# First loads of an attention and soft-MoE kernel: two q transfers from ScalarE's DMA queue, and GpSimd's first transfer ahead of the identity and the masks

## The chip, the cores and the metric

The kernel runs on one NeuronCore of a Trainium2 chip. The metric is the device time of one execution in microseconds, as the median of several runs. The engines go by the names of the profile: PE is the matrix engine (TensorE), DVE is VectorE, ACT is ScalarE, POOL is GpSimd and SP is SyncE. SP, ACT and POOL can each issue DMA transfers; a transfer that converts fp32 into fp16 on its way is issued by POOL here.

## The reference

The inputs q, k and v have the shape [8, 8, 576, 64] (batch, heads, tokens, head dimension) in fp32. First comes causal attention in a window of 64 tokens, then a soft mixture of 8 experts with 4 slots each over the 4608 tokens of width 512.

```python
# attention
scores = scale * np.matmul(q, k.transpose(0, 1, 3, 2))
mask = (rel >= 0) & (rel < window)
scores = np.where(mask, scores, -1000000000.0)
scores = scores - np.max(scores, axis=-1, keepdims=True)
attn = np.exp(scores)
attn = attn / (np.sum(attn, axis=-1, keepdims=True) + 1e-09)
x = np.matmul(attn, v)                      # then laid out as [4608, 512]
# soft MoE
logits = x @ phi                            # phi [512, 32]
d = softmax of logits over the tokens       # dispatch
slot_input = d.T @ x                        # [32, 512], 4 slots for each of 8 experts
h = np.maximum(slot_input[e] @ w1[e], 0.0)  # w1 [8, 512, 1024]
slot_out[e] = h @ w2[e]                     # w2 [8, 1024, 512]
c = softmax of logits over the slots        # combine
out = c @ slot_out                          # [4608, 512] fp32
```

## The kernel before

The whole program is written out by hand in the order in which each engine is to run it (a manual schedule); the framework adds the semaphores. Each engine works through its own queue strictly in order.

The attention goes over 32 pairs of heads (8 batches of 4 pairs). A pair p passes through a pipeline of stages in the loop `for n in range(-1, NP - 1)` at line 553:

- q and k of the pair are transposed by PE (`st_transpose`, line 316) and copied out of PSUM, k by ACT (line 327) or DVE (line 324), q by ACT (line 336), and in the very first pair half of q by DVE (line 333).
- `st_max` (lines 346 and 349) makes masked scores from which DVE takes the row maxima (line 353); `st_shift` (lines 366 and 367) turns the maxima around; `st_score` (lines 372 and 375) makes the scores with the maxima taken off, and ACT takes the exponential (line 381).
- `st_av` (line 405) multiplies by v, DVE normalises (line 415), and the result is transposed again (lines 429 and 433) for the logits, the softmax over tokens that runs along from batch to batch, and the slot inputs.

After the last pair come the two layers of the experts (`first`, line 816, and `second` and `second_last`, lines 837 and 846), in two halves of 256 output columns. The second half of line 846 needs `w2h`, the last weights to be loaded. Then the output is put together from the combine weights, scaled by ACT and DVE (lines 899 and 897), and written by SP in 14 transfers (line 901).

**The loads.** POOL issues nearly all of them, each one converting fp32 into fp16: k and q in groups of four heads (`load_k`, `load_q`, line 79, group g), v (line 173), and the weights of the experts one by one in between (lines 133, 135, 142, 150 and 155). Their order is written out: `load_k(1)` at line 121, then `load_q(1)`, `load_v(0)`, `load_k(2)` and so on from line 194, and one or more in each step n of the loop. POOL also shifts v for the odd blocks (lines 180 and 182) and writes the 0/1 identity `ident_h` (by `make_identity`) and the two selections that make the mask block `wb` (lines 117 and 119).

The first four heads of q and k (group 0) go another way. They are loaded as fp32 by SP, in four transfers of two heads each (line 103), into memory that will hold weights only later, and are rounded to fp16 by ACT and DVE (`round_rows`, line 110). Each of the four has 96 partitions of two rows of 1536 bytes. The order of issue is k pair 0, q pair 0, k pair 1, q pair 1, and behind them SP issues phi (line 254). The rounding is spread over two engines: ACT rounds k of pair 0 and q of pair 1, DVE rounds q of pair 0 and k of pair 1. On DVE the order is: q of pair 0, the two copies that make `wm` from the mask block (line 233), k of pair 1 and then its half of q (line 333).

ACT's own work begins with the load of its function table, put ahead of its first copy, which writes `lh` (line 211). That copy reads `db`, which DVE makes from the identity (lines 205 to 209).

Of the kernel before, what the change touches and what calls it, by code (L numbers as in the profile page):

```python
# [18 lines left out]
def kernel(  # L19
# [10 lines left out]
    nc = tc.nc  # L30
# [37 lines left out]
    RP = S // RQ  # L68
# [6 lines left out]
    def load_rows(src, g, tag, pairs=(0, 1)):  # L75
        t = pin.tile([128, 4, RQ * Dh], FP16, name=tag, tag=tag)
        b, gq = divmod(g, 2)
        h0, nh = 4 * gq + 2 * pairs[0], 2 * len(pairs)
        nc.gpsimd.dma_start(out=t[0:RP, 0:nh, :],  # L79
                            in_=src[b].rearrange("h (p r) d -> p h (r d)", p=RP)[:, h0:h0 + nh, :])  # L80
        for i, pr in enumerate(pairs):
            staged[tag, 2 * g + pr] = t, 2 * i

    def load_k(g):
        load_rows(k, g, "ks")
# [14 lines left out]
    for i, (src, tag, pr) in enumerate(((k, "ks", 0), (q, "qs", 0), (k, "ks", 1), (q, "qs", 1))):  # L100
        f = w1_t[5 - i // 2, 0][:, :, :].rearrange("p c f -> p (c f)").bitcast(FP32)
        f = f[0:RP, 768 * (i % 2):768 * (i % 2) + 768].rearrange("p (h x) -> p h x", h=2)
        nc.sync.dma_start(out=f, in_=src[0].rearrange("h (p r) d -> p h (r d)", p=RP)[:, 2 * pr:2 * pr + 2, :])
        if pr == 0:
            staged[tag] = pin.tile([128, 4, RQ * Dh], FP16, name=tag, tag=tag)
        first_rows[tag, pr] = f
        staged[tag, pr] = staged[tag], 2 * pr

    def round_rows(tag, pr, copy):
        copy(out=staged[tag][0:RP, 2 * pr:2 * pr + 2, :], in_=first_rows[tag, pr])  # L110

    ident_h = const.tile([128, 128], FP16, name="ident_h")
    nc.vector.memset(ident_h, 0.0)
    wb = const.tile([64, 128], FP16, name="wb")
# [3 lines left out]
                            base=0, pattern=[[1, 128]], channel_multiplier=-1)  # L118
    nc.gpsimd.affine_select(out=wb, in_=wb, compare_op=ALU.is_ge, fill=NEG,
                            base=64, pattern=[[-1, 128]], channel_multiplier=1)  # L120
    load_k(1)


    def w1_dram(e):
# [552 lines left out]
    b, p = B - 1, NP - 1  # L677
# [273 lines left out]
```

## Time and profile before

| | us |
|---|---|
| median of 3 runs | 191.47 |
| lowest and highest run | 191.35, 192.05 |
| profiled execution, whole time | 191.22 |
| profiled execution, span from first to last instruction | 189.4 |
| busy in the span: PE | 160.4 |
| busy in the span: ACT | 144.9 |
| busy in the span: DVE | 142.9 |
| busy in the span: POOL | 98.5 |

The span is what the profile's views count in; the rest of an execution's time lies around it. The mean TensorE clock that was granted is 0.974 of full speed. In the timeline, each line has the start in us, the duration in us, the engine, the line of the kernel, the operation with what it writes and reads, how often it was merged, and in brackets how long the engine had been idle before it and what ended that wait. In the view of busy time by stage a line has the stretch, its length, the busy time of PE, PE's weight loads, DVE, ACT and POOL with the number of instructions, and then the clock, the mean share of the 16 DMA engines' time that packets took (above 1 where packets overlap on an engine) and the rate in GB/s. In the view of DMA queues, a line has the number of packets that started in the stretch, their megabytes, and the time they took as a share of 16 engines' time; `hardware_dynamic` is the queue that SP issues to, `software_dynamic` POOL's.

### The profile page before, as it was taken

What the parts mean: (1) busy time and instruction counts of PE and PEld (TensorE: products, weight loads), DVE (VectorE), ACT (ScalarE), POOL (GpSimd) and SP (SyncE); (2) the same over time, 40 slices, a digit from 0 to 9 for tenths busy, and PEclk for the clock granted to TensorE, in tenths of its full rate; (3) what the DMA queues carried; (4) which work ended last, traced back from release to release, by engine and by line L of the source; (5) the groups of instructions that cost most, each with busy time, mean ns of one, the idle gap of its engine ahead of it and who ended that gap; (6) DMA issues with size and microseconds to landing.
All of it is one profiled execution on the core that took longest, in us unless ns stands there. A gap on an engine that the chain in (4) does not pass through costs nothing. (4 is left out here: it accounts for less than half of the span.)

```text
span 189.4 us, 7060 instructions
## 1 busy us (share of the span) xinstructions
PE 160.4 (85%) x3036; PEld 120.5 (64%) x3036; DVE 142.9 (75%) x352; ACT 144.9 (76%) x266; POOL 98.5 (52%) x123
## 2 busy tenths in 40 slices
PE   5787999999999999999999899999989897769500
PEld 1466878877777777777777787776774365633100
DVE  6798796897888889788878988888886555289800
ACT  6487879989889898988999898988588256379600
POOL 7857927273695554983984828727854160000000
PEclk9999999999999999999999999999999999999955
DMA  6999999999999999999999999999999999979996
GB/s 153 222 184 185 226 175 223 179 223 179 185 226 180 210 192 184 207 196 185 210 195 192 211 182 198 199 204 195 213 214 212 204 196 179 277 258 422 415 415 252
DMA packets 61630, 41.47 MB, mean 219 GB/s; under 512 B 38816, under 2 KB 57504, under 8 KB 60704
## 3 DMA queue, kind: packets, MB, share of 16 engines
q0 software_dynamic: 56560, 30.35, 116.1%
q1 hardware_dynamic: 5040, 10.68, 15.9%
q8 instruction: 23, 0.38, 0.7%
q14 instruction: 7, 0.06, 0.1%
HBM read 61.93 MB, written 9.44 MB: 377 GB/s over the span
## 5 line engine op out<-in xcount | busy, mean ns | idle before, releaser
L336 ACT ACTIVATE qb<-a_q 64x576 f16<-64x576 f16 x63 | 40.6, 645 | 5.5 <-PE a_q L316 4.0
L353 DVE TENSOR_REDUCE m<-a_m 128x8 f16<-128x1024 f32 x32 | 39.2, 1224 | 1.0
L381 ACT ACTIVATE pt<-a_s 128x1024 f16<-128x1024 f32 x32 | 32.8, 1024 | 6.6 <-PE a_s L375 5.4
L180 POOL COPY v<-v 64x1152 f16<-64x1152 f16 x16 | 18.3, 1142 | 32.8 <-DMA v<-in_v_dram 32.6
L415 DVE TENSOR_TENSOR x_b<-a_v,rc 128x640 f16<-128x640 f32 x31 | 25.6, 825 | 1.1
L349 PEld LDWEIGHTS <-qb 128*128 128x128 f16 x256 | 16.8, 98 | 7.8 <-ACT qb L336 0.4
L346 PE MATMUL a_m<-wm,ident_h 128*128 128x512 f16 x64 | 19.3, 384 | 0.9 <-DVE m L353 0.9
L375 PEld LDWEIGHTS <-lh 128*128 128x128 f16 x288 | 18.8, 98 | 1.9 <-issue 1.7
L173 POOL DMA_DIRECT2D v<-in_v_dram x16 | 19.8, 1235 | 0.0
L372 PEld LDWEIGHTS <-kT 128*128 128x128 f16 x288 | 18.6, 98 | 1.6 <-issue 1.4
L372 PE MATMUL a_s<-qb,kT 128*128 128x128 f16 x256 | 19.5, 219 | 0.0
L349 PE MATMUL a_m<-kT,qb 128*128 128x128 f16 x256 | 19.5, 219 | 0.0
L375 PE MATMUL a_s<-rt,lh 128*128 128x128 f16 x256 | 19.5, 219 | 0.0
L433 ACT COPY xt<-a_k 128x576 f16<-128x576 f16 x28 | 17.9, 640 | 2.0 <-PE a_k L429 0.7
L182 POOL COPY v<-v 64x1088 f16<-64x1088 f16 (+1 forms) x16 | 17.9, 1120 | 0.8
L405 PE MATMUL a_v<-v,pt 128*64 128x65 f16 x558 | 15.6, 196 | 2.1 <-DVE m L363 1.1
L897 DVE TENSOR_SCALAR w<-cp,rcs 128x512 f32<-128x512 f32 (+1 forms) x22 | 12.9, 635 | 5.7 <-PE cp L892 5.4
L367 DVE CAST rt<-a_v 9x128 f16<-9x128 f32 x30 | 8.7, 289 | 11.0 <-PE a_v L366 10.7
L327 ACT ACTIVATE kT<-a_k 128x576 f16<-128x576 f16 x24 | 15.7, 654 | 0.8 <-PE a_k L316 0.8
L405 PEld LDWEIGHTS <-pt 128*64 128x64 f16 x576 | 13.5, 110 | 4.3 <-DVE m L363 1.8
L79 POOL DMA_DIRECT2D ks<-in_k_dram x15 | 10.4, 696 | 10.9 <-PE a_s L375 3.0
L316 PE MATMUL a_q<-ident_h,qs 96*64 96x96 f16 x384 | 14.7, 206 | 1.6 <-DVE a_q L225 1.3
(182 smaller groups left out, 332.6 us busy)
## 6 DMA issues: line engine op xcount, KB each, us to landing
w<-in_moe_w_dram POOLq DMA_DIRECT2D x13, 1024.0 KB, 16.8
out_dram<-w SPq DMA_DIRECT2D x9, 768.0 KB, 6.2
v<-in_v_dram POOLq DMA_DIRECT2D x16, 288.0 KB, 12.4
ks<-in_k_dram POOLq DMA_DIRECT2D x15, 288.0 KB, 15.2
qs<-in_q_dram POOLq DMA_DIRECT2D x15, 288.0 KB, 12.5
out_dram<-w SPq DMA_DIRECT2D x2, 640.0 KB, 4.4
w1h<-in_moe_w_dram POOLq DMA_DIRECT2D x4, 256.0 KB, 15.9
w<-in_moe_w_dram POOLq DMA_DIRECT2D x4, 256.0 KB, 14.8
```

The lines of the kernel that those rows point to most:

```text
L173: nc.gpsimd.dma_start(out=v1s[b % 2][:, c, 0:Dh], in_=v[b].rearrange("h s d -> (h s) d").rearrange("(c p) d -> p c d", p=128)[:, c, :])
L180: nc.gpsimd.tensor_copy(out=v2[64:128, c0:c1, 0:Dh], in_=v1[0:64, c0:c1, 0:Dh])
L182: nc.gpsimd.tensor_copy(out=v2[0:64, c0:c1, 0:Dh], in_=v1[64:128, c0 - 1:c1 - 1, 0:Dh])
L336: nc.scalar.activation(qbs[p % NQ][h, :, hf, :], turned(a_qh)[h], AF.Copy, scale=QKS)
L346: nc.tensor.matmul(a_m[:, j, :], ident_h[:, :], wm[:, j:j + 4, :].rearrange("p c x -> p (c x)"), start=True, stop=False, skip_group_check= ...
L349: nc.tensor.matmul(a_m[:, i // 4, 128 * (i % 4):128 * (i % 4) + 128], qblock(p, i), kwindow(p, i), start=False, stop=True, skip_group_chec ...
L353: nc.vector.reduce_max(ms[p % 2][:, 64:72].rearrange("p (l c) -> p l c", l=2), a_m[:, :, :].rearrange("p l (c x) -> p l c x", x=128), axis ...
L372: nc.tensor.matmul(at(i), kwindow(p, i), qblock(p, i), start=(i % 4 == 0), stop=False, skip_group_check=True)
L375: nc.tensor.matmul(at(i), lh[:, i, :], rt[:, :], start=False, stop=True, skip_group_check=True)
L381: nc.scalar.activation(st_pt(p)[:, 0:8, :].rearrange("p i x -> p (i x)"), a_s[:, :, :], AF.Exp, scale=XS)
L405: nc.tensor.matmul(a_v[r0:r0 + 64, hf, 65 * (i // 2):65 * (i // 2) + 65], pt[:, i, 64 * hf:64 * hf + 64], rhs, start=True, stop=True, skip ...
L415: nc.vector.tensor_tensor(out=xbs[b][:, :, 128 * hp:128 * hp + 128].rearrange("p c (l d) -> p l c d", l=2), in0=avv[:, :, :, 0:64], in1=rc ...
```

## The change

The two transfers of q in the first group are issued by ACT instead of SP. The two of k stay on SP, and so does phi behind them. `load_k(1)`, POOL's first transfer, moves from behind the identity and the two mask selections to ahead of them. On ACT the two issues stand ahead of the load of the function table; all other instructions keep their order on each engine.

```diff
     for i, (src, tag, pr) in enumerate(((k, "ks", 0), (q, "qs", 0), (k, "ks", 1), (q, "qs", 1))):
         f = w1_t[5 - i // 2, 0][:, :, :].rearrange("p c f -> p (c f)").bitcast(FP32)
         f = f[0:RP, 768 * (i % 2):768 * (i % 2) + 768].rearrange("p (h x) -> p h x", h=2)
-        nc.sync.dma_start(out=f, in_=src[0].rearrange("h (p r) d -> p h (r d)", p=RP)[:, 2 * pr:2 * pr + 2, :])
+        eng = nc.sync if tag == "ks" else nc.scalar
+        eng.dma_start(out=f, in_=src[0].rearrange("h (p r) d -> p h (r d)", p=RP)[:, 2 * pr:2 * pr + 2, :])
...
+    load_k(1)
     ident_h = const.tile([128, 128], FP16, name="ident_h")
     nc.vector.memset(ident_h, 0.0)
...
     nc.gpsimd.affine_select(out=wb, in_=wb, compare_op=ALU.is_ge, fill=NEG,
                             base=64, pattern=[[-1, 128]], channel_multiplier=1)
-    load_k(1)
```

## The prediction, made before the changed kernel ran

> **What bounds the kernel now.** I read the page first, then the busy time by stage, then the waits and the timeline of the two ends. The chain of waits on the page is no help here: it covers only the last 13 us and ends in the output.
>
> ```profile
> span 189.4 us, 7060 instructions
> ...
> DMA  6999999999999999999999999999999999979996
> ...
> q0 software_dynamic: 56560, 30.35, 116.1%
> ...
> HBM read 61.93 MB, written 9.44 MB: 377 GB/s over the span
> ```
>
> The DMA row is at 9 in every slice but the first and the last few: the transfers hardly ever rest. q0 is GpSimd's queue (all q, k, v after the first quads, and all weights), q1 is SP's. The view by stage shows the same from inside: in the two stages below DMA share stays above 1 and the rate near 198 GB/s, while PE is busy for 19.2 and 18.8 of 20 us.
>
> ```profile
> 20.00:40.00 20.00, 19.21 (x412) 16.05 (x411) 16.29 (x46) 17.63 (x30) 10.35 (x12) 1.00 1.39 198
> ...
> 80.00:100.00 20.00, 18.84 (x401) 15.31 (x400) 16.67 (x41) 18.02 (x33) 14.67 (x18) 1.00 1.44 195
> ```
>
> So two lines run side by side for 160 us: GpSimd's stream of transfers and the compute chain. The tail of the timeline shows which one ends last:
>
> ```profile
> 162.69 0.28 PE L846 MATMUL op<-w2h,hT 128*32 128x256 f16 x2
> 163.75 0.29 PE L846 MATMUL op<-w2h,hT 128*32 128x256 f16 x4 [0.78 <-DMA w2h<-in_moe_w_dram]
> ```
>
> PE waits 0.78 us for the last weights. It is the only wait of PE on a transfer in the whole run. After it come 189.4 - 163.75 = 25.65 us of output, which nothing in the change touches. The end therefore moves by the later of two things: the stream (weights at 163.75) and the compute chain (ready at 162.97). If the stream gains X and the chain gains Y, the span falls by the smaller of X and Y + 0.78. Both must gain for a gain; a loss of the chain up to 0.78 is free only if X is not negative.
>
> The start, by the timeline:
>
> ```profile
> 0.73 1.28 ACT L211 ACT_TABLE_LOAD   x1 [0.73 <-PEq L935]
> 0.74 0.38 SPq L103 DMA_DIRECT2D w<-in_k_dram  x1
> 1.17 0.44 SPq L103 DMA_DIRECT2D w<-in_q_dram  x1
> ...
> 2.05 0.84 POOL L79 DMA_DIRECT2D ks<-in_k_dram  x1
> ...
> 4.15 0.83 ACT L110 CAST ks<-w 96x768 f16<-96x768 f32 x1 [0.85 <-DMA w<-in_k_dram]
> ...
> 5.57 0.56 DVE L110 CAST qs<-w 96x768 f16<-96x768 f32 x1 [1.32 <-DMA w<-in_q_dram]
> ...
> 7.11 0.86 DVE L110 CAST ks<-w 96x768 f16<-96x768 f32 x1
> 8.01 0.76 DVE L333 TENSOR_SCALAR qb<-a_q 64x576 f16<-64x576 f16 x1
> ...
> 8.79 0.83 ACT L110 CAST qs<-w 96x768 f16<-96x768 f32 x1 [1.48 <-DMA w<-in_q_dram]
> ```
>
> Call the four first transfers k0, q0, k1, q1 in SP's order. Three casts show a wait for their transfer. The third, of k1 at 7.11, shows none, but the view of line 103 gives 3.4, 4.9 and 6.6 us from issue to landing as least, median and most, and the issue table 4.4 as the median of the two k: k0 took 3.4, so k1 took 5.4, and 1.65 + 5.4 = 7.05. k1 lands just as DVE is free for it. Behind its cast DVE has line 333, for which the first maxima of PE wait (8.82).
>
> **The change, part by part.**
>
> *Two q transfers leave SP's queue.* q0's issue moves from 1.17 to about 0.74, q1's from 2.15 to 1.19, k1's from 1.65 to 1.17, phi's from 2.64 to 1.65. What the transfers gain depends on how two queues are served. The packets of the hardware queue in 1.5 to 3, 3 to 5 and 5 to 6.5 us (with GpSimd's first ones in the last), and then both queues in 7 to 7.5:
>
> ```profile
> q1 hardware_dynamic: 220, 0.32, 72.9%
> ...
> q1 hardware_dynamic: 328, 0.47, 103.3%
> ...
> q1 hardware_dynamic: 205, 0.29, 91.2%
> q0 software_dynamic: 55, 0.04, 19.1%
> ...
> q0 software_dynamic: 106, 0.08, 103.8%
> q1 hardware_dynamic: 73, 0.03, 35.1%
> ```
>
> One transfer has 96 x 2 = 192 packets. Counted along these rows (even within a row) the 192nd starts at 2.8, the 384th at 4.0, the 576th at 5.2, the 768th about 6.6. The landings 4.15, 5.57, 7.05, 8.79 come 1.35, 1.57, 1.85 and 2.2 us later. From 3 us on the 16 engines are full, so a second queue can add nothing there; it can only fill the 27% that are free before 3 us: 220/0.729 - 220 = 82 packets, worth 0.5 us at 328 in 2 us. The first packet does not come earlier, so I take half, 0.25 us. What does change is the order: k0 now shares with q0, and k1 with q1. k0 and q0 are both done at packet 384: 4.0 - 0.25 + 1.57 = 5.3. That is 1.15 late for k0 and 0.25 early for q0. k0's chain on ACT and PE (casts, transposes, line 327, line 336 ending at 7.31) has 0.7 us until DVE's line 333 at 8.01, and the latter will be later anyway.
>
> k1 is what decides. If packets still go out in order of issue it lands at 7.05. At equal shares it is done with q1, at packet 768: 6.6 - 0.25, plus about 0.3 for GpSimd's earlier packets (next part), plus 2.0 to 2.2 of lag, 8.75. The last row shows two queues served side by side, 106 packets against 73, so I go nearer to that end: 8.3, which is 1.2 late. DVE then casts k1 at 8.3, line 333 starts at 9.2, the first maxima at 10.0, and all behind them on PE follow: q1's transposes (9.67), ACT's line 336 (10.16) and the second maxima (11.52). q1 itself lands a little earlier than 8.79, but its transposes stand behind the first maxima on PE. PE is busy for 19 of 20 us later, so the chain cannot make this good. Y = -1.2, between -1.7 (equal shares) and +0.4 (k1 0.4 earlier).
>
> [...]
>
> *ACT issues two transfers ahead of its table load.* 2 x 0.45 (SP's issues) move the load from 0.73 to 1.63, to end at 2.9; the copy of lh (1.15) ends at 4.2 instead of 3.3. Cover: the cast of k0, at 4.15 before and 5.3 now. Without it, 0.05 to 0.9 on a chain with 0.7 of slack: nothing in the sum.
>
> *GpSimd's first issue goes ahead of the identity.* GpSimd sat idle 0.76 us until 1.20 for DVE's memsets; the issue (0.84) starts at about 0.74 and ends at 1.58, so the identity is 0.38 late (1.58 to 1.87), just in time for DVE's line 205 at 1.94, and DVE has 1.32 us idle before q0's cast. The masks end at 2.46, before line 229 at 3.50. The next issues (2.88 and on) come 0.46 earlier, the first 1.31 earlier. GpSimd's first packets came at about 5.1, 3 us after the issue; now at 3.8, among the hardware queue's. What the stream gains: low end 0, if it only takes turns with the rest; high end 1.31, the whole move. In 6.5 to 7, still beside hardware packets, it ran 72 in 0.5 us; 1.31 us at that rate are 189 packets, which at its later 138 in 0.5 us are worth 0.68 us. X = 0.7. The hardware queue loses some 0.3 us by it, counted above.
>
> *Sum.* Smaller of X = 0.7 and Y + 0.78 = -0.42: the span grows by 0.42 us, to 189.8. The profiled run took 191.22 in all, 1.8 over its span, and the median of three is 191.47; so 191.47 + 0.42 = 191.9, a change of 0.2%. A measurement of this kernel can tell about 0.5% (0.96 us) from no change, so this is no change.
>
> **Rivals.**
>
> *The two queues add up (faster).* For it: between 2.5 and 3 us the hardware queue alone moved over 350 GB/s, far above its 235 after 3 us, so the engines can do more than one queue later draws from them. Against it: 103% busy in 3 to 5. At the 129 packets per 0.5 us of that half microsecond, 768 packets take 3 us from 1.9, 5.6 with GpSimd's share; with 1.2 to 1.6 of lag k1 and q1 land near 6.8. DVE's cast of k1 then starts 0.3 to 0.4 early: Y = +0.4, X = 1.3, gain 1.18: 190.3.
>
> *The start gets worse than shared (slower).* The drop from 350 to 235 GB/s at 3 us comes just as GpSimd's first issue ends (2.89). If the one causes the other, the issue at 0.74 puts the slow rate on k0 from its first packet: 45 to 60 packets fewer by 3 us, 0.35 late, on top of equal shares, and 0.3 more from GpSimd's packets: k1 at 9.4, Y = -2.4, loss 1.6: 193.1. It decides from Y below -1.74 on, where the loss passes 0.96. Against it: after 7 us the queue runs beside GpSimd's issues without such a drop.
>
> *It does not do what it says (same).* Packets are served in order of issue whichever queue they stand in: k1 0.2 late by GpSimd's packets, X = 0.7, gain 0.58: 190.9. [...]
>
> **How the numbers follow.** Forecast 0.30 (within 0.5% in 0.24 of it, slower in 0.06; its own range 191.3 to 192.5), two queues add up 0.27 (faster 0.23, same 0.04), worse start 0.26 (slower 0.24, same 0.02), no effect of the queue 0.17 (same 0.13, faster 0.04). Faster 0.27, same 0.43, slower 0.30. The range reaches to both outer cases: 190.2 to 193.1.
>
> **What would show it.** Right: k0's cast near 5.3, q0's near 5.3, k1's cast showing a wait for its transfer and starting near 8.3; first maxima near 10.0; line 846 with no wait for w2h, or a shorter one. Wrong: k1's cast at 7.1 or before, or w2h waited for longer than 0.78, which would mean that the chain gained or the stream lost. The forecast also falls if the lateness of the start is made good before 150 us.

## The result, and the profile after

| | before | changed |
|---|---|---|
| median of 22 runs each | 191.75 us (191.35 to 192.79) | 193.42 us (191.26 to 197.22) |
| profiled execution: whole, span | 191.22, 189.4 | 194.1, 192.3 |

The ratio of the times is 1.0047, with a 95% interval of 1.0029 to 1.0066; ratios, and counts of executions called kept, leave out executions that lie over 1.5% above the fastest of their kernel, here 6 of the changed kernel's 22, with spans of 191.5 to 195.1. By the ratio the kernel is slower by about 0.9 us, just inside the bound of 0.5% and with an interval across it. The plain median lies 0.9% higher and outside the predicted range.

The median hides what happened. The 16 executions that were kept have spans in two groups: 8 at 189.5 to 190.2 us, where those of the kernel before lie, and 8 at 191.4 to 192.3. The 102 executions of the kernel before that ran beside the experiments below have spans of 189.0 to 191.2, half of them below 189.9 and only three at 191.0 or above. So the change costs nothing in 8 of the 22 executions and 1.5 us or more in the other 14; the profiled execution, 2.9 us longer than the profiled one of before, is one of the latter.

The start, in the changed kernel's timeline, ACT and then DVE:

```profile
0.73 0.92 ACTq L104 DMA_DIRECT2D w<-in_q_dram  x2
1.69 1.28 ACT L212 ACT_TABLE_LOAD   x1 [1.69 <-PEq L936]
2.98 1.15 ACT L212 COPY lh<-db 64x1152 f16<-64x1152 f16 x1
4.97 0.83 ACT L111 CAST ks<-w 96x768 f16<-96x768 f32 x1 [0.84 <-DMA w<-in_k_dram]
...
8.30 0.82 ACT L111 CAST qs<-w 96x768 f16<-96x768 f32 x1
```

```profile
5.41 0.68 DVE L111 CAST qs<-w 96x768 f16<-96x768 f32 x1 [0.47 <-DMA w<-in_q_dram]
...
7.25 0.72 DVE L111 CAST ks<-w 96x768 f16<-96x768 f32 x1
8.43 0.76 DVE L334 TENSOR_SCALAR qb<-a_q 64x576 f16<-64x576 f16 x1 [0.45 <-ACT qb L337]
```

k0 is cast at 4.97 instead of 4.15, q0 at 5.41 instead of 5.57. k1 shows no wait: it was issued at 1.17 and needed 6.1 us by the view of line 104, so it landed near 7.2, some 0.2 late, not 1.2. Line 334 waits for line 337 on ACT, for q0's chain, not for k1. PE shows where that comes from, the changed kernel first, then the kernel before, at the same instructions:

```profile
5.86 0.69 PE L317 MATMUL a_k<-ident_h,ks 96*64 96x96 f16 x12 [1.15 <-ACT ks L111]
6.48 0.61 PE L191 MATMUL a_m<-v 128*128 128x512 f16 x1
7.02 0.69 PE L317 MATMUL a_q<-ident_h,qs 96*64 96x96 f16 x12
...
9.23 1.03 PE L347 MATMUL a_m<-wm,ident_h 128*128 128x512 f16 x2
10.05 1.00 PE L350 MATMUL a_m<-kT,qb 128*128 128x128 f16 x8
```

```profile
5.03 0.69 PE L316 MATMUL a_k<-ident_h,ks 96*64 96x96 f16 x12 [0.33 <-ACT ks L110]
5.66 0.39 PE L190 MATMUL a_m<-v 128*128 128x512 f16 x1
6.18 0.45 PE L316 MATMUL a_q<-ident_h,qs 96*64 96x96 f16 x12
...
8.41 0.60 PE L346 MATMUL a_m<-wm,ident_h 128*128 128x512 f16 x2
8.85 0.61 PE L349 MATMUL a_m<-kT,qb 128*128 128x128 f16 x8
```

In the kernel before, PE's instructions become 1.5 to 1.7 times faster at 5.66 us: twelve transposes take 0.45 us instead of 0.69. In the changed kernel they stay at the slow durations until 10.86. The clock column of the view by stage shows 1.00 for these first stretches in both kernels, so here the durations alone tell; in a later slow stretch of the same execution column and durations agree (clock 0.50 from 17.7 to 21.1 us). Below, "slow PE" means these durations; the expectations call them half rate. With PE slow, 0.82 us of lateness in k0 becomes 1.30 us at the first maxima. DVE behind them, and GpSimd beside it, in the changed kernel:

```profile
11.10 1.23 DVE L354 TENSOR_REDUCE m<-a_m 128x8 f16<-128x1024 f32 x1 [0.91 <-PE a_m L350]
...
12.55 1.00 DVE L268 TENSOR_TENSOR lh<-lh,db 64x64 f16<-64x64 f16 x1
13.47 0.22 DVE L241 COPY rt<-db 64x128 f16<-64x128 f16 x1
13.72 0.95 DVE L242 COPY rt<-ident_h 64x64 f16<-64x64 f16 x1
...
18.38 1.17 DVE L242 COPY rt<-ident_h 64x64 f16<-64x64 f16 x1
```

```profile
12.33 1.14 POOL L181 COPY v<-v 64x1152 f16<-64x1152 f16 x1 [0.66 <-DMA v<-in_v_dram]
13.53 1.11 POOL L183 COPY v<-v 64x1088 f16<-64x1088 f16 x1
...
18.37 1.14 POOL L181 COPY v<-v 64x1152 f16<-64x1152 f16 x1
```

And DVE in the kernel before, at the same lines (one less each), with GpSimd's first copy of v:

```profile
9.80 1.22 DVE L353 TENSOR_REDUCE m<-a_m 128x8 f16<-128x1024 f32 x1
...
11.25 0.22 DVE L267 TENSOR_TENSOR lh<-lh,db 64x64 f16<-64x64 f16 x1
11.39 0.22 DVE L240 COPY rt<-db 64x128 f16<-64x128 f16 x1
11.65 0.17 DVE L241 COPY rt<-ident_h 64x64 f16<-64x64 f16 x1
11.74 0.17 DVE L242 COPY rt<-ident_h 64x64 f16<-64x64 f16 x1
...
12.68 1.14 POOL L180 COPY v<-v 64x1152 f16<-64x1152 f16 x1
```

Three small operations (two copies and the addition on `lh`; below, small copies for short) that take 0.17 to 0.22 us by themselves take 0.95 to 1.17. Each starts while GpSimd copies v and ends 0.03 to 0.08 us behind that copy: 13.55 against 13.47, 14.67 against 14.64, 19.55 against 19.51. In the kernel before, the first four small copies are through at 11.91, ahead of GpSimd's first copy at 12.68. A lateness of 1.3 us pushes them into it, and it becomes 2.85 at the second maxima (15.99 against 13.14). The work that ACT does at 17.5 us in the kernel before comes 3.79 us later, and what it does there at 159 us still 3.64.

The other end, PE at the last weights in the changed kernel:

```profile
166.03 0.28 PE L847 MATMUL op<-w2h,hT 128*32 128x256 f16 x2
166.14 0.28 PE L847 MATMUL op<-w2h,hT 128*32 128x256 f16 x2
166.34 0.38 PE L847 MATMUL op<-w2h,hT 128*32 128x256 f16 x4
```

No wait: the last weights landed at 163.76, against 163.71 before. The stream gained nothing, and the chain came 3.64 us later, of which the old wait covers 0.78: 189.4 + 3.64 - 0.78 = 192.3, the measured span.

### The profile page after: what moved, and what is told of

The parts are those of the page before. It is cut to its first block, busy times and chain, and to the rows that moved or that the text cites. A ratio compares the mean times of both kernels' runs of the same rounds, so it can differ in the third digit from the quotient of the medians.

```text
span 192.3 us, 7060 instructions
## 1 busy us (share of the span) xinstructions
PE 163.3 (85%) x3036; PEld 122.3 (64%) x3036; DVE 144.8 (75%) x352; ACT 144.9 (75%) x266; POOL 98.4 (51%) x123
## 5 line engine op out<-in xcount | busy, mean ns | idle before, releaser
L350 PEld LDWEIGHTS <-qb 128*128 128x128 f16 x256 | 17.7, 101 | 8.1 <-ACT qb L337 0.5
L347 PE MATMUL a_m<-wm,ident_h 128*128 128x512 f16 x64 | 19.8, 391 | 1.2 <-DVE m L354 1.2
L350 PE MATMUL a_m<-kT,qb 128*128 128x128 f16 x256 | 20.4, 225 | 0.0
L317 PE MATMUL a_q<-ident_h,qs 96*64 96x96 f16 x384 | 15.3, 211 | 1.4 <-DVE a_q L226 1.3
```

The costliest lines, as they stand in the source:

```text
L347: nc.tensor.matmul(a_m[:, j, :], ident_h[:, :], wm[:, j:j + 4, :].rearrange("p c x -> p (c x)"), start=True, stop=False, skip_group_check= ...
L350: nc.tensor.matmul(a_m[:, i // 4, 128 * (i % 4):128 * (i % 4) + 128], qblock(p, i), kwindow(p, i), start=False, stop=True, skip_group_chec ...
```

## The experiments

In each profile I took k0's cast on ACT, how far ACT's cast of line 904 (158.74 us before) came behind the kernel before, and the landing of the last weights. The rule of the prediction then gives a span: 189.4 plus the larger of that lag less 0.78 and the lateness of the weights against 163.71. The end of the first slow stretch is read from PE's durations, that of a later one from the clock column; with "by", PE was idle when it changed and fast at its next work.

| kernel | k0's cast | slow PE until | lag | weights | rule | span | median, ratio to before (95%) |
|---|---|---|---|---|---|---|---|
| before | 4.15 | 5.66 | 0 | 163.71 | 189.4 | 189.4 | |
| changed | 4.97 | 10.9 | 3.64 | 163.76 | 192.3 | 192.3 | 193.42, 1.0047 (1.0029 to 1.0066) |
| changed, again | 5.16 | 12.8 | 2.92 | 163.63 | 191.5 | 191.6 | one run, 193.36 |
| only ACT's queue | 5.00 | 13.2 | 3.20 | 163.86 | 191.8 | 191.8 | 193.63, 1.0052 (1.0009 to 1.0096) |
| only GpSimd's move | 4.23 | 10.8 | 0.90 | 163.69 | 189.5 | 189.4 | 192.18, 1.0029 (0.9997 to 1.0060) |
| q first on SP | 5.40 | 10.9 | 2.85 | 163.62 | 191.5 | 191.3 | 192.46, 1.0043 (1.0013 to 1.0073) |
| quads split | 4.73 | by 5.6, again 8.5 to 11.9 | 1.68 | 164.05 | 190.3 | 190.0 | 193.34, 1.0037 (1.0004 to 1.0070) |
| short warm-up | 4.10 | 11.5 | 0.90 | 163.88 | 189.6 | 189.6 | 191.64, 0.9986 (0.9957 to 1.0014) |
| long warm-up | 4.95 | 5.56 | 0.49 | 163.66 | 189.4 | 189.6 | 191.85, 1.0020 (0.9993 to 1.0046) |
| copies early | 5.10 | by 5.98, again 12.2 to 15.6 | 1.89 | 163.78 | 190.5 | 190.5 | 191.68, 0.9999 (0.9980 to 1.0017) |
| both | 4.90 | 5.0 | 0.84 | 163.71 | 189.5 | 191.4 | 192.59, 1.0033 (1.0000 to 1.0066) |
| both, again | 4.88 | 5.3, again 12.1 to 15.5 | 1.87 | 163.64 | 190.5 | 190.5 | 192.03, 1.0020 (0.9988 to 1.0052) |
| lighter stream | 3.98 | 11.3 | 0.46 | 162.53 | 189.1 | 188.9 | 190.94, 0.9944 (0.9910 to 0.9977) |
| before, copies early | 4.04 | 5.6 | 0.51 | 163.42 | 189.1 | 189.1 | 191.60, 0.9998 (0.9974 to 1.0021) |

In all but one of them the rule is right within 0.3 us. A single profile is one execution of several that are possible, so for the question of what brings the late executions the spans of all runs count as much.

**Half of the change each.** The kernel before with only the two q transfers on ACT's queue:

```diff
-        nc.sync.dma_start(out=f, in_=...)
+        eng = nc.sync if tag == "ks" else nc.scalar
+        eng.dma_start(out=f, in_=...)
```

> The changed kernel with GpSimd's order as before; only the two q transfers go through ACT. Theory A (the late first k transfer leaves PE idle for over 1 us after its warm-up, PE then runs at half rate until about 10.9 us, and the chain that is 1.4 us late by then meets GpSimd's copies): this part alone does it, k0 is cast near 4.9 us instead of 4.15, the median is 192.5 to 194 and single runs lie 2 us and more apart. Theory B (the prediction's: sharing puts the first k transfers late, and that alone is the loss): 191.9 to 192.4, little spread. Theory C (GpSimd's move is what costs): 191.5, as before.

And with only GpSimd's first issue moved:

```diff
+    load_k(1)
     ident_h = const.tile([128, 128], FP16, name="ident_h")
...
-    load_k(1)
```

> The changed kernel with all four first transfers on SP; only GpSimd's first transfer goes ahead of the identity. A and B: k0 cast near 4.15 us as before, PE idle 0.3 to 0.5 us after its warm-up, 191.3 to 191.7. C: the identity 1 us late and the stream's descriptors in the way of the first transfers, 192.5 or more. Whether the stream gains from the earlier issue: by the prediction the last weights land 0.7 us earlier than 163.7; if GpSimd's packets wait until the hardware queues are empty, at 163.7 as before.

ACT's queue alone does all of it: k0's cast at 5.00, slow PE, three small copies of 0.95 to 1.14 us, lag 3.20, and five of its eight kept executions at 191.6 to 192.0. GpSimd's move alone leaves k0 nearly where it was (4.23). It lets GpSimd's packets in among SP's from 4.9 us on, q1 is cast at 10.18 instead of 8.79, and the first maxima are read at 10.79. Its spans run from 189.4 to 191.5, a little above those before; the interval reaches 1.0060, so a small cost is neither shown nor excluded. The stream gains nothing by it either: the last weights land at 163.69.

How two hardware queues share shows in the DMA view of the changed kernel (packets, megabytes, share of the 16 engines; q1 is the queue that SP issues to, q10 ACT's), first in 3 to 3.5 us, then in 4.5 to 5:

```profile
q1 hardware_dynamic: 59, 0.09, 47.9%
q10 hardware_dynamic: 58, 0.09, 47.1%
...
q1 hardware_dynamic: 66, 0.10, 94.4%
q10 hardware_dynamic: 13, 0.02, 17.3%
```

In the first stretch, with k0 and q0 on their way, the two are served alike; in the second SP's queue is far ahead, and k1 with it. From 2 to 3 us the sum is lower than SP's queue alone had moved: 39 and 57 packets in the two halves, against 60 and 129 in the kernel before. By 5 us both kernels have moved about the same.

**Only a late k0, with no second queue.** The first two transfers on SP are exchanged.

```diff
-    for i, (src, tag, pr) in enumerate(((k, "ks", 0), (q, "qs", 0), (k, "ks", 1), (q, "qs", 1))):
+    for i, (src, tag, pr) in enumerate(((q, "qs", 0), (k, "ks", 0), (k, "ks", 1), (q, "qs", 1))):
```

> The kernel before with the first two transfers of SP's queue exchanged: q's first quad, then k's. No second hardware queue, and GpSimd's order as before; k's first quad is late alone, by one quad's service (1.0 to 1.4 us: its cast at 5.1 to 5.6 instead of 4.15), and q's early (4.1 to 4.2). If the late first quad of k is what costs: PE's idle time behind the warm-up 1.3 to 1.9 us, half rate to 10 us or later in most executions, and a tail of executions at 191.4 us of span and above as with the change, so that the median is 192.3 to 193.5. Rival, that the cost is in the use of two hardware queues: 191.6 to 192.0 us, spans of 189.0 to 190.6.

The profile repeats that of the changed kernel. PE and DVE in it:

```profile
6.29 0.69 PE L316 MATMUL a_k<-ident_h,ks 96*64 96x96 f16 x12 [1.58 <-ACT ks L110]
```

```profile
12.76 0.59 DVE L267 TENSOR_TENSOR lh<-lh,db 64x64 f16<-64x64 f16 x1
13.27 0.22 DVE L240 COPY rt<-db 64x128 f16<-64x128 f16 x1
13.52 0.95 DVE L241 COPY rt<-ident_h 64x64 f16<-64x64 f16 x1
...
18.17 1.17 DVE L241 COPY rt<-ident_h 64x64 f16<-64x64 f16 x1
```

Slow PE and the same three long copies, lag 2.85, and a ratio of 1.0043. So neither the second queue nor ACT's two issues nor GpSimd's move are needed; an order of transfers that makes k0 late is enough. The group of late executions is smaller, though: 3 of the 11 kept, at 191.3 to 191.5, and all 11 are at 189.8 or above.

**k0 on time with two queues.** The first quads of k and of q are each cut in two halves by head, one on each queue.

```diff
...
+        if pr == 0:
+            nc.sync.dma_start(out=f[:, 0:1], in_=x[:, 0:1])
+            nc.scalar.dma_start(out=f[:, 1:2], in_=x[:, 1:2])
+        else:
+            eng = nc.sync if tag == "ks" else nc.scalar
+            eng.dma_start(out=f, in_=x)
```

> The changed kernel, but the first quads of k and of q are each split by head in two halves, one on SP's queue and one on ScalarE's, so that k's first quad again has both queues to itself. If the loss begins with the late first quad of k: its cast near 4.2 to 4.5 us instead of 4.97, PE's idle time behind the warm-up 0.3 to 0.6 us instead of 1.15, ScalarE's lag 0.8 us or less from 20 us on, span 189.4 to 189.9, and no group of executions at 191 us and above that before does not have: 191.6 to 192.0. Rival, that a second hardware queue or GpSimd's earlier issue costs by itself: span 191.5 or more and 193 to 193.5 us, as in the changed kernel. The last weights land at 163.6 to 163.9 in either case.

This missed: it doesn't bring k0 back. Its halves landed at 4.48 and 4.71 instead of 4.13, and ACT's copy of `lh` now ends at 4.59. From 2 to 3 us the two queues together moved 51 packets, where SP's alone moved 189 in the kernel before; by 3.5 us SP's queue had started more than the 96 packets of its half of k, ACT's 65 of its 96. So the slow start of two queues makes k0 late even when it has both, and SP's queue goes on to q while ACT's is still at k. PE idled for 0.91 us, one small copy took 1.06, the profiled lag was 1.68, and two of the seven kept executions are at 191.5 and 191.6. So the late group is there with k0's cast 0.58 us late instead of 0.82. What a timely k0 does with two queues stays untested.

**PE's idle time and the slow stretch.** The changed kernel with `warm_up(9)` instead of `warm_up(6)`, so that PE has work until k0 is there:

```diff
-    warm_up(6)
+    warm_up(9)
```

> The changed kernel with 9 instead of 6 warm-up matmuls, so that PE is busy until about 6 us. A: PE is at full rate 2 to 5 us earlier, the chain is late by less than 0.8 us, the span falls back to about 189.5 and the time to 191.3 to 191.8 with little spread. B and C: as the changed kernel, median near 193.4, since neither the transfers nor GpSimd's order change.

And the kernel before with `warm_up(3)`, which makes the idle time with k0 on time:

```diff
-    warm_up(6)
+    warm_up(3)
```

> The kernel before with 3 instead of 6 warm-up matmuls and no change to any transfer: PE idles from 3.3 to about 5.0 us. A (PE's idle gap and half rate are the first link): k0 cast at 4.15 as before, yet PE at half rate to 8 us or later, the first maxima 0.8 to 1.4 us late, and executions spread up to spans of 191 to 192, median 192 to 193.5. B (the transfers' lateness itself): 191.5, as before, since every transfer lands as before.

With nine, PE is at its faster durations from 5.56 on, k0 as late as ever (4.95); the profiled execution has no long copy ahead of 15 us, the lag is 0.01 us at 20 us, and seven of ten executions are at 189.6 to 190.2. Three are still at 191.1 to 191.6, so the little spread that was expected did not come. The reverse was expected to reproduce the loss and didn't:

```profile
11.82 0.22 DVE L267 TENSOR_TENSOR lh<-lh,db 64x64 f16<-64x64 f16 x1
11.96 0.22 DVE L240 COPY rt<-db 64x128 f16<-64x128 f16 x1
12.21 0.17 DVE L241 COPY rt<-ident_h 64x64 f16<-64x64 f16 x1
12.30 0.17 DVE L242 COPY rt<-ident_h 64x64 f16<-64x64 f16 x1
```

```profile
12.32 1.16 POOL L180 COPY v<-v 64x1152 f16<-64x1152 f16 x1 [0.72 <-DMA v<-in_v_dram]
```

PE idled for 1.56 us and stayed slow to 11.5, which made the chain 1.05 us late. But the first three copies were done and the fourth had just begun when GpSimd's copy started at 12.32. They escaped by hundredths of a microsecond, and the lag fell back to 0.58 at the second maxima. A slow PE alone costs about 1 us here, most of which the 0.78 covers; with k0 late on top it is 1.3 to 2.0, and the copies are hit.

PE's idle time does not decide whether PE stays slow. PE's first transposes in the run with the copies early (below), then in the run with GpSimd's move alone:

```profile
5.98 0.45 PE L316 MATMUL a_k<-ident_h,ks 96*64 96x96 f16 x12 [1.28 <-ACT ks L111]
```

```profile
5.11 0.69 PE L316 MATMUL a_k<-ident_h,ks 96*64 96x96 f16 x12 [0.41 <-ACT ks L110]
```

After 1.28 us of idle time PE is fast at once, after 0.41 it is slow and stays so to 10.8. The split (0.91, fast) and the lighter stream (0.16, slow to 11.3) say the same. So theory A's first link, from the idle time to the slow PE, is not borne out: a late k0 and a slow PE are two things, and three copies are hit only in the four profiles in which they come together (changed, changed again, only ACT's queue, q first). What makes PE slow in one execution and not in another stays open.

**The small copies out of the way.** The changed kernel with the copies that make `rt` and the sum on `lh` moved up, ahead of GpSimd's copies of v:

```diff
     round_rows("ks", 1, nc.vector.tensor_copy)
...
+    make_rt(rts[1])
...
             zero_q(1)
-        elif n == 1:
             nc.vector.tensor_tensor(out=lh[64:128, 0, 0:64], ...)
             make_rt(rts[0])
+        elif n == 1:
             nc.vector.memset(ms[1], 0.0)
             zero_q(2)
-        elif n == 2:
-            make_rt(rts[1])
```

> The changed kernel with DVE's small copies (rt 0 and 1, and the addition to lh) put ahead of the second maxima, before GpSimd's first copies of v at 12.3 us. A, and that DVE's copies of 0.2 us took 1.0 us because GpSimd's copies ran: none of them over 0.3 us, chain lag 1.4 to 2.0 us instead of 3.7, span 190 to 190.6 and time 191.9 to 192.6, PE still at half rate until about 10.9 us. If the long copies are not what adds to the lag: median near 193.4.

The last of the first four small copies, and GpSimd's first copy of v:

```profile
10.88 0.17 DVE L243 COPY rt<-ident_h 64x64 f16<-64x64 f16 x1
...
12.31 1.14 POOL L181 COPY v<-v 64x1152 f16<-64x1152 f16 x1 [0.68 <-DMA v<-in_v_dram]
```

No copy is long any more, and the late group is gone: ten of ten executions are at 189.6 to 190.6, ratio 0.9999, with k0 as late as in the changed kernel (5.10). These ten spans are the strongest evidence that the lost time is made where DVE's copies meet GpSimd's, and not by the 0.8 us of k0 itself. The profile says less, since the slow PE that was expected until 10.9 did not come in it. It lost 1.1 us in another way: PE stood idle for 1.55 us, because the first maxima now stand behind the copies on DVE, and was slow from 12.2 to 15.6. All four profiles with the copies early have this idle time; in two of them PE was slow behind it.

Both remedies together, twice:

> The changed kernel with both remedies: 9 warm-up matmuls, and DVE's small copies early. A: chain lag under 0.5 us, no small copy over 0.3 us, all executions at spans of 189.3 to 190.2, median 191.4 to 191.8 with no tail. It can't be faster than before, because the stream ends at 163.7 us in every run so far. If the earlier landing of the last first transfer (7.7 instead of 8.8 us) is worth something of its own: 190.9 or less.

> The kernel with nine warm-ups and the copies early once more. Its profile lost nothing ahead of 160 us beyond the 0.78 us that the wait for the weights covers (lag 0.84), ended its last ScalarE instruction when before did, and still was 2 us longer; in it one 16 KB packet of the instruction queue fell at 183.4 us, amid the last output transfers, where before has none behind 164 us but one of 8 KB. If that packet held up one DMA engine: wherever a packet of 16 KB falls between 166 and 187 us the span is 191 us or more with ScalarE's last instruction near 178.8; without it 189.4 to 189.8. Rival, that the kernel loses time ahead of 160 us: ScalarE's lag there over 0.8 us by as much as the span grows.

The first time this missed altogether. ACT was 0.84 us late at 159 us and within 0.01 us of the kernel before at its last instruction, and still the span was 191.4. The loss lay behind all computing. The DMA engines from 188 to 190 us, where the kernel before has nothing left to move (forty slices, busy share in tenths):

```profile
DMA  0020000200002000200002000200002000000000
```

Never more than 2 tenths, in even steps: 12 packets in 2 us, which take 5.3% of the 16 engines' time, about that of one engine (16 x 0.053 = 0.85). In 183 to 184 us the view of that execution has a packet of another kind among the output's:

```profile
q1 hardware_dynamic: 65, 0.40, 97.0%
q8 instruction: 1, 0.02, 5.9%
```

It is one packet of 16 KB of instructions that takes 0.94 us (5.9% of 16 engines in 1 us), as long as four output packets of 0.24; of its queue this execution has 24, where every other profile has 23, that of the same kernel the second time too. The second time there was none between 164.2 and 191.5 us, and the rule holds again: lag 1.87, 190.5. That fits a held-up engine, but 0.94 us is half of the 1.9 us that were lost; the rest wasn't found. Of the 20 executions of this kernel four are at 191.3 to 191.8, and only one of these four was profiled, so whether the early copies leave a late group when PE starts fast is open.

**The rule itself, from the other side.** The kernel before without the last group's load of q, whose four heads use the q of the group before, so that this part isn't computed:

```diff
+        if g == NG - 1:
+            for pr in range(2):
+                staged["qs", 2 * g + pr] = staged["qs", 2 * g - 2 + pr]
+            return
```

> The kernel before without the last group load of q (288 KB of GpSimd's stream; the last four heads use the q of the group before, so this part of the result is not computed). The rule that the span falls by the smaller of the stream's gain and the chain's gain plus 0.78: the last weights land 1.3 to 1.5 us earlier, at about 162.3, PE no longer waits for them, and the span falls by 0.6 to 0.8 to about 188.7, time 190.7 to 191.0. If the stream is not what sets the end: 191.5.

And the kernel before with the small copies early:

> The kernel before, with the small copies of VectorE (line 265 on) moved ahead of GpSimd's copies of v, as in the run with the changed kernel. It takes away the one long small copy of before (0.92 us at L240). If the span falls by the smaller of the stream's gain and of the chain's gain: the chain comes 0 to 0.8 us earlier, PE waits longer for the last weights (0.8 to 1.6 us instead of 0.78), the weights land at 163.7, span 189.2 to 189.6, 191.7 us. Rival, that the chain alone sets the end: span lower by all that ScalarE gains, down to 188.7.

The first lands the last weights 1.18 us earlier, at 162.53, and the span falls by 0.5: now the chain, 0.46 us late in that execution but with 0.78 to spare, ends last. Of all kernels here it alone has an interval wholly below 1. The second left the time where it was (0.9998) and did not make the chain earlier: it was 0.51 us late in the profile, and the span of 189.1 goes with weights that landed 0.29 us earlier, at 163.42, and a chain that had 0.27 to spare.

**The changed kernel again**, to see whether the profile of the late group repeats:

> The changed kernel once more, for one more profile. A: if its span is near 189.6, PE got its full rate before 8 us or DVE's small copies missed GpSimd's; if it is near 191.6, PE is at half rate until about 11 us or more and at least one small copy took near 1 us. In both, span = 189.4 + chain lag - 0.78, and not under 189.4.

The same three copies are long (0.75, 0.95, 1.15 us), the slow stretch ends at 12.8 instead of 10.9, and the lag is 2.92 instead of 3.64. PE has no second slow stretch from 17.7 us on here, so most of the lag doesn't need it.

## Why the prediction was right and wrong

*The model was right.* The span as the later of two lines, with 0.78 us to spare for the chain, gives 12 of the 13 other profiles within 0.3 us when the measured lag and landing are put in. The lateness of the start was not made good in 150 us, as the prediction argued from PE's 19 busy microseconds in 20.

*k0 and q0: right in direction, a little large.* k0's cast was said for 5.3 and came at 4.97 (4.97 to 5.16 in the changed kernel and its copies early), q0's at 5.41 for 5.3. Equal shares are shown by 59 against 58 packets. The 0.25 us that a second queue was to gain ahead of 3 us did not come: from 2 to 3 us the two moved 96 packets, where one had moved 189.

*k1: mis-sized, and the wrong carrier.* The prediction has "k1 is what decides", 1.2 us late. It landed some 0.2 late. The step that failed is that k1 shares equally with q1 and is nearly as late as packet 768: from 4.5 to 5 us SP's queue moved 66 packets and ACT's 13, so that k1's last packet started near 5.5 us, with about 650 started in all. GpSimd's first packets, counted for 0.3 us of delay, were not among them yet. Why ACT's queue fell behind there is not shown. q1 landed 1.1 us early, at 7.67. The first maxima were nevertheless 1.3 us late (11.10 instead of 9.80; "near 10.0" was expected), by way of k0: "k0's chain on ACT and PE has 0.7 us until DVE's line 333" was reckoned with PE's durations of before. In this execution PE kept its slow ones until 10.86, and the 0.7 us were gone.

*Y: -1.2 said, -3.64 in the profile.* The step that failed is that a late start is carried on as it is. It is not: it moved DVE's small copies onto GpSimd's copies of v, an overlap that the profile of before shows was missed by 0.8 us. Where none of GpSimd's copies of v was met, the lateness was carried on roughly as it was: 0.99 us at the first maxima and 0.90 at 159 us with GpSimd's move alone, 0.56 and 0.46 with the lighter stream. The prediction listed what stands behind k1's cast on DVE and PE, but not what GpSimd does at the same time.

*X: +0.7 said, about 0 measured.* GpSimd's first issue started at 1.31, not at 0.74, behind 0.86 us of its own queue, and its first packets came at 6.3 us instead of 5.1, although the issue was 0.74 us earlier. The second hardware queue does that: with GpSimd's order as before and only the q transfers on ACT's queue they came at 6.5. In the run with GpSimd's move alone they came at 4.9, and q1 paid: from 5.5 to 6.5 us GpSimd's queue moved 186 packets and SP's 30. In the kernel before, SP's queue alone kept the 16 engines at 92 to 113% from 2.5 to 5 us, which fits that one queue gains what the other loses; X is the low end that the prediction named, 0. The last weights landed at 163.6 to 163.9 in every kernel with one stream of transfers as long as before, but for the split (164.05) and one execution (163.42).

*The rivals.* That the start gets worse than shared gave 193.1, near the late executions, but its mechanism, GpSimd's early issue slowing k0, didn't occur: with GpSimd's move alone k0's cast is at 4.23, and with ACT's queue alone it is as late (5.00) as with both. In the changed kernel none of GpSimd's packets came before 6.3 us. That the queue does nothing fell with k0's cast. Two queues that add up fell with 57 packets in the half microsecond that had 129.

So 191.9 is right for the executions of the lower group only, and the ratio of 1.0047 is a mean of those and of a group that the prediction did not foresee. The forecast of no change came out by the share of the groups, which is luck, and not by its sum.

## What to carry to other kernels

A transfer that the first work of TensorE waits for should go first and alone: here a second queue brought the pair of k0 and q0 in 0.15 us earlier, and the first of the two 0.8 us later. Before a start is allowed to slip by a microsecond, look at what other engines do in the microsecond behind each short VectorE copy, and move such copies away from GpSimd's long ones first: in the changed kernel that alone took out the late group, in ten executions. And where two lines end within 0.8 us of each other, a gain on the one that ends last is worth at most that margin and a gain on the other nothing, so ask first whether both move.

## What the runs showed of the hardware

The time at which PE becomes fast differs between executions and kernels that start alike: 5.66 us in the kernel before, 10.8 in the run with GpSimd's move alone and 11.3 with the lighter stream, though k0 came at 4.23 and 3.98 there. In the changed kernel's execution the edges lie at 10.86, 17.69 and 21.10, so 6.83 and 3.41 us apart; the later slow stretches of the three other executions that have one took 3.4 us too (8.5 to 11.9, 12.2 to 15.6 and 12.1 to 15.5, in the table). What sets these edges no view here shows, so that their position divides the executions into two groups is possible and not shown.

VectorE's small fp16 copies and the one addition on them, where they started behind the start of a GpSimd copy, ended 0.03 to 0.08 us behind its end in the four profiles that have three long ones. One that had just started kept its length (in the changed kernel line 241 from 13.47 for 0.22 us, with GpSimd's copy from 13.53); and the reduction from PSUM kept its length beside them: in the kernel before, line 353 takes 1.23 us at 13.14, beside GpSimd's copies from 12.68 on, and 1.22 without one at 9.80. The kernel before has one such long copy too: its copy of line 240 at 15.26 took 0.92 us and ended at 16.18, with GpSimd's issue of a transfer of v (14.92 to 16.15), not with a copy. Beside GpSimd's copies of v the long ones took 0.37 us (0.59 instead of 0.22, with q first on SP) to 1.0 us (1.17 instead of 0.17, in the changed kernel) more than by themselves; why, no view here shows.

What stays open: the executions with spans above 194 us, of which none was profiled (3 of 22 in the changed kernel, 1 of 10 with only ACT's queue, 4 of 12 with the split and 1 of 12 with q first, none in any other kernel); the second microsecond of the one long output; and why the exchanged order gives fewer late executions than the second queue, at the same lag in the profile.
